# Scores ahead of a step's second layer, products with v behind it, in a two-bank buffer; two alternating banks for the first layer

## The chip, the cores and the metric

The kernel runs on one core of one Trainium2 chip. The metric is the device time of one execution in microseconds (us); lower is better. The kernel before is given by the median of three timed runs and by one further execution, from which the profile was taken.

## What is computed

The inputs are q, k and v of shape (batch 8, heads 8, sequence 576, head size 64) in float32, a norm vector of 512 and two feed-forward matrices of 512 x 2048 and 2048 x 512. Cut to what matters, the reference is:

```python
scores = q @ k.transpose(0, 1, 3, 2) / sqrt(64)
# heads 0-3: a query sees itself and the 31 keys before it
# heads 4-7: a query sees every earlier key whose position has the same remainder mod 32
attn = softmax(where(mask, scores, -1e9))
x = (attn @ v).transpose(0, 2, 1, 3).reshape(8, 576, 512)
xn = (x - mean(x)) / sqrt(var(x) + 1e-6) * g_ln
out = x + relu(xn @ w1) @ w2
```

## The kernel before

The 4608 tokens are cut into nine chunks of 512: chunk c < 8 is the first 512 tokens of batch entry c, and chunk 8 collects the last 64 tokens of all entries. The attention works on 32 "pairs" of two heads of one batch entry. Pairs with an even index are strided, those with an odd index local. The masks leave few blocks: a local pair has 18 score blocks for each head, each 32 queries by 64 keys; a strided pair has 11 for each head, each 64 rows by 54. These small float32 products run on tiles of TensorE (64 x 32 and 64 x 64), not on the full 128 x 128 array.

The first eight pairs are computed at the start, with chunk 0, in an order written out by hand (`ORDER`). Then comes the stretch that the change touches: chunks 1 to 6, each of 16 steps, 96 in all. Step f of chunk c does this in program order:

- **First layer**, `ffn1`: 12 matmuls of 128x128 by 512 columns into the PSUM bank `ph` (lines L802 and L809). There is one such bank, in the pool `ps_h`.
- ScalarE makes `hh` from `ph` (L814), then VectorE makes `hl` from `ph` and `hh` (L819). These two hold the first layer's result as a high and a low part.
- **One turn of the generator** `pieces()`, which threads the attention of the remaining 24 pairs through the steps.
- **Second layer**, `second(*prev)`: 12 matmuls (L829) with the `hh` and `hl` of the step before, into four banks `po` that a chunk holds for 16 steps. At step 0 the second layer ends the chunk before, and VectorE adds the residual (L835).

For i from 7 to 31 the generator makes a *visit*, of three steps where `short` holds and of four otherwise. `now` is pair i and `nxt` is pair i + 1. In the visit's first step `m_piece` runs: TensorE computes the scores of `nxt` (L445) and then, directly behind them, the product of `now`'s weights with v (L514). Both go into one buffer `m` of three banks. VectorE adds the mask (L473), takes the row maxima (L486), divides the product by its sums (L564); SyncE stores it; GpSimd subtracts the maxima (L491) and ScalarE takes the exponential (L497). The buffer is laid out so that head 0 and head 1 never use the same bank at the same time: for that the last score block of a strided pair lies in the third bank, the v products of head 0 lie in the third bank, and those of head 1 at the ends of the first two. The mask is added in three parts (strided) or two (local), the division is done in five.

In the visit's second step `x_raw` loads the stored output back in 32-column slices (ScalarE's queue, L593), `v_sums` makes the row sums (L534 to L536), `p_turned` turns the exponentials in 32x32 blocks and sends them to DRAM (L610, L614, buffer `pd`), `t_piece` turns the next raw q and k (L415, L416, L420), and `load_qk` fetches raw q and k of a later pair (L356). In the third step `p_load` brings the turned exponentials back as `pt` (L623 or L628; for a short visit with a strided `nxt` this stands in the second step, on SyncE's queue), and `x_blocks` turns `xraw` and splits it into the high and low part of the next chunk's x (L602, L685, L686).

Each engine runs its instructions in program order (a loop at the end of the kernel ties each to the one before it on its engine). The first visit has scores only, the last one products only; 24 visits have both. In chunk 6 a table `last_steps` adds work for the last two chunks at given steps: loads of the tail tokens, transposes and splits.

Of the kernel before, what the change touches and what calls it, by code (L numbers as in the profile page):

```python
# [8 lines left out]
F32 = mybir.dt.float32  # L9
# [53 lines left out]
def kernel(  # L63
# [10 lines left out]
    nc = tc.nc  # L74

    B, H, S, D = q.shape
    DM, DFF = w1.shape
    P = 128
# [5 lines left out]
    NL = (NB + 3) // 4  # L84
# [3 lines left out]
    CH = 512  # L88
# [20 lines left out]
    ps_h = ctx.enter_context(tc.tile_pool(name="ps_h", bufs=1, space=bass.MemoryType.PSUM))  # L109
# [198 lines left out]
    banks = [(ps_a, "a", 1024)]  # L308
    n_bank = [0]

    def bank(name):
        pool, tag, n = banks[n_bank[0] % len(banks)]
        n_bank[0] += 1
        return pool.tile([P, n], F32, tag=tag, name=name)

    def halves(ps, n, w):

        return ps.rearrange("p (h x) -> p h x", h=2)[:, :, 0:n * w].rearrange(
            "p h (t x) -> p h t x", x=w)
# [6 lines left out]
    class Pair:  # L326
# [97 lines left out]
        def s_blocks(self, ps):  # L424

            nt, w = self.nt, (64 if self.local else GS)
            wide = ps.shape[1] > 1024 and not self.local

            def at(h, t):
                o = 1024 + D * NL if wide and h == 0 and t == nt - 1 else 512 * h + w * t  # L430
                return ps[:, o:o + w]

            def block(n, h):
                rows = slice(64 * h, 64 * h + 64)
                if self.local:
                    t, jj = divmod(n, 4)
                    o = at(h, t)[STR * jj:STR * (jj + 1)]
                    lhsT = self.qt[rows, STR * n:STR * (n + 1)]
                    rhs, pos = self.kt[rows, STR * n:STR * n + 64], STR * jj
                else:  # L440
                    t, c = divmod(n, 2)
                    o = at(h, t)[64 * c:64 * c + 64]
                    lhsT = self.qt[rows, GS * n:GS * n + 64]
                    rhs, pos = self.kt[rows, GS * n:GS * (n + 1)], 64 * c
                nc.tensor.matmul(o, lhsT, rhs, start=True, stop=True, tile_position=(64 * h, pos))  # L445

            if self.local:
                n = 4 * NL if self.full else NB
            else:
                n = 2 * NS if self.full else NG  # L450
            for i in range(n):
                for h in range(2):
                    block(i, h)

            sv = halves(ps[:, 0:1024], nt, w)
            parts = [(r, 0, 2, t0, t1, sv[r, :, t0:t1]) for r, t0, t1 in self.parts]
            if wide:
                r = parts[1][0]
                parts[1:] = [(r, h, h + 1, nt - 1, nt, at(h, nt - 1)[r].rearrange(
                    "p (h t x) -> p h t x", h=1, t=1)) for h in range(2)]  # L460
            return parts

        def s_masked(self, parts):
            self.s_mask(parts)
# [73 lines left out]
        def v_blocks(self, ps):  # L538

            nt = self.nt  # L540

            def o(h, t):
                return 1024 + D * t if h == 0 else 512 * (t // 3) + 512 - D * (3 - t % 3 if t < 3 else nt - t)

            for i in range(NB if self.local else NG):
                for h in range(2):
                    self.v_block(i, h, lambda h, t: ps[:, o(h, t):o(h, t) + D], D)
            r = self.parts[1][0]
            parts = []
            for h, rs, t0, t1 in ((1, slice(0, P), 0, 3), (1, slice(0, P), 3, nt - 1), (1, r, nt - 1, nt),  # L550
                                  (0, slice(0, P), 0, nt - 1), (0, r, nt - 1, nt)):
                parts.append((rs, h, h + 1, t0, t1, ps[rs, o(h, t0):o(h, t0) + D * (t1 - t0)].rearrange(
                    "p (h t d) -> p h t d", h=1, d=D)))
            return parts

        def v_divide(self, parts):
            nt = self.nt
# [109 lines left out]
                nc.vector.tensor_tensor(  # L667
                    out=lo, in0=src, in1=hi.bitcast(F32), op=ALU.subtract)

    def m_piece(p, nxt):  # L670

        ps = bank(f"m{(p or nxt).id}")
        parts = nxt.s_blocks(ps) if nxt else None
        av = p.v_blocks(ps) if p else None
        if nxt:
            nxt.s_masked(parts)
        if p:
            p.v_divide(av)
            p.v_store()
        if nxt:  # L680
            nxt.s_sub()
            nxt.s_exp()

    def split_x(hi, lo, src):
        nc.scalar.activation(out=hi, in_=src, func=AF.Copy)  # L685
# [108 lines left out]
    def ffn1_high(c, f, ccs=range(NCC), ph=None):  # L794
        xh, xl = xt[c]
        new = ph is None
        if new:
            ph = ps_h.tile([P, CH], F32, tag="h", name=f"ph{c}_{f}")
        w1h = w1s[f][:, 0].rearrange("p (c f) -> p c f", c=NCC)
        for n, cc in enumerate(ccs):  # L800
            for i, x in enumerate((xh, xl)):
                nc.tensor.matmul(  # L802
                    ph, w1h[:, cc], x[:, cc, :], start=(new and n == 0 and i == 0), stop=False)
        return ph
# [18 lines left out]
    def ffn2(c, f, h, po):  # L823
        hh, hl = h
        w2h, w2l = (w2s[f][:, i] for i in range(2))
        for i in range(NT):
            cs = slice(i * P, (i + 1) * P)
            for n, (hx, w) in enumerate(((hh, w2h), (hh, w2l), (hl, w2h))):
                nc.tensor.matmul(  # L829
                    po[i], hx[:, cs], w,  # L830
                    start=(f == 0 and n == 0), stop=(f == NFC - 1 and n == 2))
# [15 lines left out]
    def second(c, f, h, xres):  # L847
        nonlocal po
        if f == 0 and c == NCHUNK - 1:
            po = [pool.tile([P, DM], F32, tag=tag, name=f"po{c}_{i}") for i, (pool, tag) in  # L850
                  enumerate(((ps_l, "x2"), (ps_h, "h"), (ps_l, "x3"), (ps_l, "x4")))]
        elif f == 0:
            po2 = [ps_o[i].tile([P, 1024], F32, tag="o", name=f"po{c}_{i}") for i in range(NT // 2)]
            po = [po2[i // 2][:, DM * (i % 2):DM * (i % 2 + 1)] for i in range(NT)]
        ffn2(c, f, h, po)
        if f == NFC - 1:
            finish(c, po, xres)
# [4 lines left out]
    ps, ph, hs, splits = {}, {}, {}, {}  # L862
# [143 lines left out]
    def pieces():  # L1006
        for i in range(2 * NHP - 1, NP):
            now = pairs[i] if i >= 2 * NHP else None
            nxt = pairs[i + 1] if i + 1 < NP else None
            short = i < 3 * NHP - 1 or i in (25, 27, 29)  # L1010
            m_piece(now, nxt)
            if i + 2 < NP:
                pairs[i + 2].load_v()
            yield
            if now:
                now.x_raw(nc.scalar)
            if nxt:
                nxt.v_sums()
                nxt.p_turned()
                if short and not nxt.local:  # L1020
                    nxt.p_load(nc.sync)
            if i + 2 < NP:
                pairs[i + 2].t_piece()
            if i + 3 < NP:
                pairs[i + 3].load_qk()
            yield
            if nxt and not (short and not nxt.local):
                nxt.p_load(nc.scalar)
            if now and now.b == B - 1:
                cc = now.h0 // 2  # L1030
                if cc >= NHP // 2:
                    whole_tile(0, (f"b21{cc % 2}", f"b11{cc % 2}"))
                now.x_blocks(whole[f"b{1 + cc // 2}1{cc % 2}"])
            elif now:
                now.x_blocks()
            yield
            if not short:
                yield

    gen = pieces()  # L1040
    RES_AT = 4, 5, 7, 8
    ps_r_ctx.close()
    ps_m_ctx = ExitStack()
    ps_m = ps_m_ctx.enter_context(tc.tile_pool(name="ps_m", bufs=1, space=bass.MemoryType.PSUM))
    banks[:] = [(ps_m, "m", 1536)]


    def tail(cc):
# [6 lines left out]
    wide = NCHUNK - 2  # L1055
# [44 lines left out]
    for c in range(1, wide):  # L1100
        xres = []
        for f in range(NFC):
            ph = ffn1(c, f)
            hh = h_high(c, f, ph)
            h = hh, h_low(c, f, ph, hh)
            next(gen, None)
            if c == wide - 1:
                for do in last_steps.get(f, ()):
                    do()
            second(*prev)  # L1110
            if 2 <= c < 2 + NFC // 4 and f in (2, 11):
                w_sums(2 * (c - 2) + int(f > 2))
            if 2 <= c < 2 + NFC // 4 and f in (3, 15):
                w_whole(2 * (c - 2) + int(f > 3))
            if f in RES_AT:
                xres.append([x_load(c, RES_AT.index(f))])
            if f - 3 in RES_AT:
                i = RES_AT.index(f - 3)
                xres[i].append(x_scale(xres[i][0], f"{c}_{i}"))
            prev = c, f, h, xres  # L1120
# [139 lines left out]
```

## Time and profile before

| what | value |
|---|---|
| median of three runs | 887.09 us (886.63 to 887.17) |
| the profiled execution's own time | 885.76 us |
| its span, first to last instruction | 884.0 us |
| TensorE matmul busy | 866.6 us, 98% of the span |
| VectorE busy | 484.9 us, 55% |
| ScalarE busy | 213.1 us, 24% |
| GpSimd busy | 211.4 us, 24% |
| mean granted TensorE clock | 0.998 of full speed |

The span is what the trace covers; 1.76 us of the execution's own time lie outside of it. Busy times of different engines overlap. A matmul's row is longer (about 390 ns) than the distance between two matmuls (about 227 ns), since they are pipelined, so the distance between starts, not the row's length, is what a matmul costs.

### The profile page before, as it was taken

Reading aid. Unit: us, or ns where it says so; the run is one execution under the profiler, and the core shown is the slowest. Engines: PE = TensorE matmul, PEld = TensorE weight load, DVE = VectorE, ACT = ScalarE, POOL = GpSimd, SP = SyncE. Lnnn points to the kernel's source line nnn. Section 1 sums busy time; section 2 is a strip of 40 time slices with the busy share of each in tenths; the row PEclk is TensorE's granted clock in tenths of the full one; section 3 lists DMA queues with packets and bytes.
Section 4 is the critical chain, followed back from the end, with each engine's and each line's share of the span. In section 5 each row is a group of like instructions: output and inputs, shape, how many; then the busy total and the mean of one; then the engine's idle time right before and its main releaser. Section 6 shows DMA issues by size and latency. Waiting matters only on the chain.

```text
span 884.0 us, 18492 instructions
## 1 busy us (share of the span) xinstructions
PE 866.6 (98%) x7405; PEld 712.4 (81%) x7405; DVE 484.9 (55%) x933; ACT 213.1 (24%) x351; POOL 211.4 (24%) x246
## 2 busy tenths in 40 slices
PE   7799999999999999999999999999999999999997
PEld 6588888888888888888888888888887888888886
DVE  5899975456354645455544545565564542434442
ACT  3786741111111111111111111111112221212121
POOL 5887850011030223013301302113002111121000
PEclk9999999999999999999999999999999999999999
DMA  9999754685678575856686577758774153321111
GB/s 190 197 302 264 253 110 101 127 165 130 115 190 157 117 155 137 184 121 123 131 210 126 131 137 205 138 122 162 184 135 94 48 193 112 99 85 49 52 45 47
DMA packets 368301, 124.73 MB, mean 141 GB/s; under 512 B 296404, under 2 KB 353880, under 8 KB 368216
## 3 DMA queue, kind: packets, MB, share of 16 engines
q1 hardware_dynamic: 291160, 109.46, 51.0%
q10 hardware_dynamic: 77056, 14.10, 9.0%
q8 instruction: 58, 0.95, 0.5%
q14 instruction: 27, 0.22, 0.1%
HBM read 84.90 MB, written 38.60 MB: 140 GB/s over the span
## 4 chain that ended last, share of the span: by engine, by line
PE 92%; DMA 2%; SPq 2%; DVE 2%; issue 0%; ACT 0%; POOL 0%; ACTq 0%; DVEq 0%; POOLq 0%
PE po L829 43%; PE ph L802 22%; PE ph L809 11%; PE x L1144 9%; PE m L514 2%; PE m L445 2%; SPq L401 1%; DMA v_s<-in_v_dram 1%; PE av L514 1%; DMA rows<-in_q_dram 1%; PE t L373 0%; PE px L636 0%; PE cm L286 0%; DMA pt<-pd 0%; PE s L445 0%
## 5 line engine op out<-in xcount | busy, mean ns | idle before, releaser
L829 PE MATMUL po<-w,hh 128*128 128x512 f32 x1152 | 358.9, 393 | 0.0
L829 PEld LDWEIGHTS po<-w,hh 128*128 128x128 f32 x1152 | 213.5, 188 | 45.0
L829 PE MATMUL po<-w,hl 128*128 128x512 f32 x576 | 224.3, 389 | 0.0
L819 DVE SCALAR_TENSOR_TENSOR hl<-ph,hh 128x512 fp32r<-128x512 f32 x112 | 77.2, 689 | 210.9 <-ACT hh L814 210.6
L802 PE MATMUL ph<-xh,w 128*128 128x512 f32 x444 | 174.3, 393 | 0.6 <-DVE hl L819 0.6
L802 PE MATMUL ph<-xl,w 128*128 128x512 f32 x444 | 172.9, 389 | 0.0
L814 ACT ACTIVATE hh<-ph 128x512 fp32r<-128x512 f32 x112 | 66.7, 596 | 316.0 <-PE ph L809 261.5
L829 PEld LDWEIGHTS po<-w,hl 128*128 128x128 f32 x576 | 108.1, 188 | 23.0
L809 PE MATMUL ph<-xh,w 128*128 128x512 f32 x444 | 118.9, 390 | 0.0
L491 POOL TENSOR_TENSOR sm<-sm,mx 128x640 f32<-128x640 f32 (+1 forms) x31 | 39.3, 1268 | 316.6 <-DVE mx L486 284.0
L802 PEld LDWEIGHTS ph<-xh,w 128*128 128x128 f32 x444 | 83.4, 188 | 18.3 <-DVE hl L819 1.0
L809 PEld LDWEIGHTS ph<-xh,w 128*128 128x128 f32 x444 | 83.2, 188 | 17.4
L802 PEld LDWEIGHTS ph<-xl,w 128*128 128x128 f32 x444 | 83.4, 188 | 17.0
L722 POOL TENSOR_TENSOR rs<-rs,mhalf 128x1 f32<-128x1 f32 x36 | 19.8, 549 | 231.4 <-DVE rs L721 231.3
L497 ACT ACTIVATE sm<-sm 128x648 f32<-128x648 f32 (+1 forms) x32 | 23.8, 744 | 107.5 <-POOL sm L491 107.4
L303 POOL TENSOR_TENSOR w<-r,w 128x512 fp32r<-128x512 f32 x29 | 37.9, 1315 | 7.9 <-ACT w L299 7.6
L1097 POOL TENSOR_TENSOR rings<-stage,rings 128x512 fp32r<-128x512 f32 x16 | 20.6, 1289 | 71.0 <-ACT rings L1096 71.0
L1144 PE MATMUL x<-half_t,rings 128*128 128x512 f32 x144 | 36.4, 389 | 0.0
L1144 PEld LDWEIGHTS x<-half_t,rings 128*128 128x128 f32 x144 | 27.0, 188 | 5.6
L686 DVE TENSOR_TENSOR xl<-xo,xh 128x512 fp32r<-128x512 f32 x20 | 13.8, 692 | 27.6 <-ACT xh L685 27.6
L486 DVE TENSOR_REDUCE mx<-sm 128x12 f32<-128x648 f32 (+1 forms) x32 | 26.3, 823 | 2.4
L564 DVE TENSOR_TENSOR xo<-m,den 64x64 f32<-64x64 f32 (+3 forms) x120 | 27.1, 289 | 0.0
(148 smaller groups left out, 870.7 us busy)
## 6 DMA issues: line engine op xcount, KB each, us to landing
s<-in_moe_w_ch_dram SPq DMA_DIRECT2D x32, 512.0 KB
out_dram<-x SPq DMA_DIRECT2D x32, 256.0 KB
raw<-in_q_dram SPq DMA_DIRECT2D x108, 72.0 KB
raw<-in_k_dram SPq DMA_DIRECT2D x108, 72.0 KB
wd<-w SPq DMA_DIRECT2D x24, 256.0 KB
ringa<-wd SPq DMA_DIRECT2D x24, 256.0 KB
xds<-xo SPq DMA_DIRECT2D x32, 162.0 KB
v_l<-in_v_dram SPq DMA_DIRECT2D x32, 144.0 KB
```

The lines of the kernel that those rows point to most:

```text
L303: eng.tensor_tensor(out=t[:, 1], in0=self.w[i], in1=t[:, 0].bitcast(F32), op=ALU.subtract)
L486: nc.vector.reduce_max(mx[:, :, 0:nt], sm, axis=AX.X)
L491: eng.tensor_tensor(out=sm, in0=sm, in1=mx[:, :, 0:nt].unsqueeze(3).broadcast_to([P, 2, nt, sm.shape[3]]), op=ALU.subtract)
L497: nc.scalar.activation(out=self.smv, in_=self.smv, func=AF.Exp, scale=SCALE)
L514: nc.tensor.matmul(at(h, t)[m * j:m * (j + 1)], self.p_cols(rows, t, j), self.v[rows, n, 0:w], start=True, stop=True, tile_position=(64 * ...
L564: nc.vector.tensor_tensor(out=xo[r, t0:t1, h0:h1].rearrange("p t h d -> p h t d"), in0=av, in1=den[r, h0:h1, t0:t1].unsqueeze(3).broadcast_to(
L802: nc.tensor.matmul(ph, w1h[:, cc], x[:, cc, :], start=(new and n == 0 and i == 0), stop=False)
L809: nc.tensor.matmul(ph, w1l[:, cc], xt[c][0][:, cc, :], start=False, stop=(cc == NCC - 1))
L814: nc.scalar.activation(out=hh, in_=ph, func=AF.Relu)
L819: nc.vector.scalar_tensor_tensor(out=hl, in0=ph, scalar=0.0, in1=hh.bitcast(F32), op0=ALU.max, op1=ALU.subtract)
L829: nc.tensor.matmul(po[i], hx[:, cs], w, start=(f == 0 and n == 0), stop=(f == NFC - 1 and n == 2))
L1144: nc.tensor.matmul(ps, wx, xx, start=(start and j == 0 and i == 0), stop=(j == 1 and i == 2), skip_group_check=not start)
```

## The change

The turn of the generator is split: it now takes a turn ahead of the second layer and one behind it, and a visit has six or eight such half steps instead of three or four steps. The scores of `nxt` (`s_piece`) stay between first and second layer of the visit's first step. The v products of `now` (`v_piece`), their division and store and the load of v for a later pair stand behind the second layer of that step. `p_turned`, now ahead of `v_sums`, stays ahead of the second layer of the second step, with the short strided `p_load`; `x_raw`, `t_piece` and `load_qk` go behind that step's second layer. The other `p_load` stays ahead of the second layer of the third step, `x_blocks` goes behind it.

Scores and products are two allocations, one after the other, in one buffer of two banks, head 0 in the first and head 1 in the second. The mask is then added in two parts for either kind, the division done in two. The bank that becomes free is a second bank for the first layer: from chunk 1 on odd steps use `ps_b`, even ones `ps_h`.

```diff
         def s_blocks(self, ps):
             def at(h, t):
-                o = 1024 + D * NL if wide and h == 0 and t == nt - 1 else 512 * h + w * t
-                return ps[:, o:o + w]
+                return ps[:, 512 * h + w * t:512 * h + w * (t + 1)]
...
         def v_blocks(self, ps):
             def o(h, t):
-                return 1024 + D * t if h == 0 else 512 * (t // 3) + 512 - D * (3 - t % 3 if t < 3 else nt - t)
+                return 512 * h + D * t
...
-    def m_piece(p, nxt):
-
-        ps = bank(f"m{(p or nxt).id}")
-        parts = nxt.s_blocks(ps) if nxt else None
-        av = p.v_blocks(ps) if p else None
-        if nxt:
-            nxt.s_masked(parts)
-        if p:
-            p.v_divide(av)
-            p.v_store()
-        if nxt:
-            nxt.s_sub()
-            nxt.s_exp()
+    def s_piece(p):
+        p.s_masked(p.s_blocks(bank(f"s{p.id}")))
+        p.s_sub()
+        p.s_exp()
+
+    def v_piece(p):
+        p.v_divide(p.v_blocks(bank(f"av{p.id}")))
+        p.v_store()
...
-            ph = ps_h.tile([P, CH], F32, tag="h", name=f"ph{c}_{f}")
+            ph = (ps_b if c and f % 2 else ps_h).tile([P, CH], F32, tag="h", name=f"ph{c}_{f}")
...
-            m_piece(now, nxt)
+            if nxt:
+                s_piece(nxt)
+            yield
+            if now:
+                v_piece(now)
             if i + 2 < NP:
                 pairs[i + 2].load_v()
             yield
+            if nxt:
+                nxt.p_turned()
+                nxt.v_sums()
+                if short and not nxt.local:
+                    nxt.p_load(nc.sync)
+            yield
             if now:
                 now.x_raw(nc.scalar)
-            if nxt:
-                nxt.v_sums()
-                nxt.p_turned()
-                if short and not nxt.local:
-                    nxt.p_load(nc.sync)
             if i + 2 < NP:
                 pairs[i + 2].t_piece()
...
             if nxt and not (short and not nxt.local):
                 nxt.p_load(nc.scalar)
+            yield
...
             yield
             if not short:
                 yield
+                yield
...
-    banks[:] = [(ps_m, "m", 1536)]
+    ps_m, ps_b = (ps_m_ctx.enter_context(tc.tile_pool(name=n, bufs=1, space=bass.MemoryType.PSUM))
+                  for n in ("ps_m", "ps_b"))
+    banks[:] = [(ps_m, "m", 1024)]
...
             second(*prev)
+            next(gen, None)
```

## Rows read from the trace of the kernel before

**Rows 1.** The 96 steps: length, busy us (instructions) PE, PEld, DVE, ACT, POOL, PEclk, DMA.

```profile
141.10:712.75 571.65, 570.52 (x5089) 468.93 (x5089) 302.59 (x616) 96.01 (x155) 93.45 (x101) 1.00 0.64 140
```

**Rows 2.** Waits of TensorE in that stretch: total us, times, longest us.

```profile
PE ph L802 <- DVE hl L819: 0.6, 1, 0.6
PE m L514 <- DMA pt<-pd: 0.5, 1, 0.5
```

**Rows 3.** Chain of work, a plain step, then one with scores and products: start, us.

```profile
398.57 1.81 PE ph L802 x8
...
404.01 1.81 PE ph L802 x8
405.82 0.91 PE ph L809 x4
406.73 0.84 PE m L445 x44
407.56 0.90 PE m L514 x58
408.47 2.94 PE po L829 x12
411.41 1.81 PE ph L802 x8
```

**Rows 4.** The same chain in the first visit, which has scores only.

```profile
141.10 1.81 PE ph L802 x8
...
143.81 0.84 PE m L445 x44
144.65 2.94 PE po L829 x12
147.60 1.81 PE ph L802 x8
```

**Rows 5.** The same chain in the last visit, which has products only.

```profile
675.32 0.91 PE ph L809 x4
676.22 0.90 PE m L514 x58
677.12 2.99 PE po L829 x12
680.11 1.81 PE ph L802 x8
```

**Rows 6.** Timeline of VectorE behind the scores that start at 406.66.

```profile
407.45 0.69 DVE L819 SCALAR_TENSOR_TENSOR hl<-ph,hh 128x512 fp32r<-128x512 f32 x1 [3.74 <-ACT hh L814]
408.53 0.95 DVE L473 TENSOR_TENSOR sm<-m,mask_s 128x540 f32<-128x540 f32 x3 [0.38 <-PE m L514]
...
410.33 1.06 DVE L564 TENSOR_TENSOR xo<-m,den 128x192 f32<-128x192 f32 x5
```

**Rows 7.** Timeline of SyncE's queue in a short visit with a strided `now`.

```profile
202.63 0.79 SPq L582 DMA_DIRECT2D xds<-xo  x2
203.52 5.22 SPq L401 DMA_DIRECT2D v_s<-in_v_dram  x6
210.51 1.83 SPq L614 DMA_DIRECT2D pd<-sm  x4
```

**Rows 8.** Timeline of ScalarE and its queue in that visit.

```profile
209.24 1.93 ACTq L593 DMA_DIRECT2D xraw<-xds  x4
211.27 0.60 ACT L814 ACTIVATE hh<-ph 128x512 fp32r<-128x512 f32 x1 [5.38 <-DMA xraw<-xds]
214.00 0.36 ACTq L623 DMA_DIRECT2D pt<-pd  x1
```

**Rows 9.** Timeline of VectorE at the end of that visit.

```profile
213.61 0.71 DVE L602 STREAM_TRANSPOSE xo<-xraw 128x512 f32<-128x512 f32 x1 [1.01 <-DMA xraw<-xds]
...
216.80 0.69 DVE L819 SCALAR_TENSOR_TENSOR hl<-ph,hh 128x512 fp32r<-128x512 f32 x1
```

**Rows 10.** Timeline of VectorE at a chunk's end: the four residual adds.

```profile
435.21 2.71 DVE L835 SCALAR_TENSOR_TENSOR x<-po,rs,x 128x512 f32<-128x512 f32 x4
```

More of the change, by code (lines that the diff above doesn't have):

```diff
@@ L426, in s_blocks @@
             nt, w = self.nt, (64 if self.local else GS)
-            wide = ps.shape[1] > 1024 and not self.local
             def at(h, t):
-                o = 1024 + D * NL if wide and h == 0 and t == nt - 1 else 512 * h + w * t
-                return ps[:, o:o + w]
+                return ps[:, 512 * h + w * t:512 * h + w * (t + 1)]
             def block(n, h):
@@ L453, in s_blocks @@
                     block(i, h)
[L455 to L461, printed above, removed]
+            sv = halves(ps, nt, w)
+            return [(r, 0, 2, t0, t1, sv[r, :, t0:t1]) for r, t0, t1 in self.parts]
         def s_masked(self, parts):
@@ L547, in v_blocks @@
                     self.v_block(i, h, lambda h, t: ps[:, o(h, t):o(h, t) + D], D)
[L548 to L554, printed above, removed]
+            at = halves(ps, nt, D)
+            return [(r, 0, 2, t0, t1, at[r, :, t0:t1]) for r, t0, t1 in self.parts]
         def v_divide(self, parts):
@@ L1043 @@
     ps_m_ctx = ExitStack()
-    ps_m = ps_m_ctx.enter_context(tc.tile_pool(name="ps_m", bufs=1, space=bass.MemoryType.PSUM))
-    banks[:] = [(ps_m, "m", 1536)]
+    ps_m, ps_b = (ps_m_ctx.enter_context(tc.tile_pool(name=n, bufs=1, space=bass.MemoryType.PSUM))
+                  for n in ("ps_m", "ps_b"))
+    banks[:] = [(ps_m, "m", 1024)]
     def tail(cc):
```

## The prediction

> **What bounds the kernel now.** I first read the windows view over the 96 steps that the change touches, to see whether any engine but TensorE matters there. It does not: TensorE is busy 570.52 of 571.65 us at the full granted clock, VectorE about half of it, ScalarE and GpSimd a sixth [rows 1]. Then the list of waits: TensorE waits twice in the whole stretch, 0.6 us for an `hl` and 0.5 us for a `pt`, 1.1 us together [rows 2]. That is the most that a better order of the other engines can give back. What is left to ask is how long TensorE's own work becomes, so I read the chain of work step by step. A plain step goes from 398.57 to 404.01, 5.44 us, that is 2.72 for each layer. A step with scores and products goes from 404.01 to 411.41, 7.40 us, so the small products cost 1.96 us: 0.84 for the scores, 0.90 for the products with v, and 0.22 because the second layer behind them takes 2.94 instead of 2.72 [rows 3].
>
> **The change part by part.**
>
> *Two runs of small tiles instead of one.* The same matmuls are issued, so the two runs keep their lengths. What changes is how often TensorE goes from the full array to small tiles and back: once for a visit today, twice afterwards, in 24 visits. The trace shows each run alone. The first visit has scores only: its step goes from 141.10 to 147.60, 6.50 us, 1.06 over a plain one, of which the run is 0.84 and the second layer's excess 0.22 again [rows 4]. The last visit has products only: from 675.32 to 680.11 pass 4.79 us, where a plain step needs 0.91 and 2.72, 3.63; that is 1.16 over [rows 5, 3]. Apart they cost 2.22 us, together 1.96: a visit that is split costs 0.26 more. Of this, 0.05 is the second layer of the last visit (2.99 against 2.94 us), which belongs to no entry or exit; without it 0.21. The value I take is 0.22, the excess of a full layer behind a small run, which then falls on the next step's first layer too. 24 x 0.22 = +5.3 us; ends 24 x 0.21 = 5.0 and 24 x 0.26 = 6.2. Only strided scores and local products are seen alone; I assume the same for the other kind. This work is on the engine that sets the end, and nothing covers it.
>
> By the Trainium skill, TensorEngine Tiling (Array Packing), section Key Properties, changing the tiling mode drains TensorE. Scores and products use different tilings, so by that rule a visit has three changes today (full to scores, scores to products, products to full) and four afterwards; were all priced alike at half of the 0.22 us, the split would add 24 x 0.11 = 2.6 us where the rows give 5.3.
>
> *The wait of the products for the mask.* The products now go into the same buffer as the scores and must wait until VectorE has added the mask, which today they need not. In the step shown, the scores start at 406.73 and end at 407.56; `hl` runs from 407.45 to 408.14, the mask takes 0.95 in three parts and would start right behind `hl` (today it waits 0.38 for the products) [rows 3, 6]. It would end by 409.1. The products are due 2.94 us after the scores, at 410.5. That leaves 1.4 us, so I take nothing; were VectorE later than that, the second run and all full layers queued behind it on TensorE would wait. The places with least room are the two short visits with a strided `now`, since `x_blocks` moves half a step towards the next scores and already runs without a pause into the `hl` ahead of the mask: turned at 213.61, `hl` at 216.80 [rows 9]. Today 216.80 is just when `hl` is due (0.8 us after the scores start, as in rows 6). `x_blocks` becomes later by what its data does: the output is divided behind the second layer, some 0.7 us later than today, because today the division (1.06 us in five parts) stands behind mask and maximum anyway [rows 6]. So `hl` and mask are late by 0.7 there, half of the room.
>
> *The queues that steps are moved past.* SyncE: the store and the six v loads take 0.79 and 5.22 us and stand ahead of `pd` today as well [rows 7]; starting 0.7 us later they end at about 209.4, and `pd`, which goes out at 210.51 today, is not pushed back. `p_turned` ahead of `v_sums` makes it earlier, if anything. ScalarE: `x_raw` issues at 209.24 once the store has landed and takes 1.93 us; 0.7 us later it makes the next `hh` (211.27, already held back by it today) later by about as much [rows 8]. That `hh` feeds a second layer one step, 5.4 us, later, so it costs nothing. `p_load` keeps its place, 214.00 [rows 8], while the products are due half a step, 2.7 us, later: the 0.5 us wait for `pt` goes. `t_piece` moves half a step in the text, but VectorE is in order and has nothing in between except the row sums, so it hardly moves. At a chunk's end the division now stands behind four residual adds, 2.71 us [rows 10]; these start when the second layer ends, as the products do, so the division comes some 2 us later there, still ahead of the next `hl`.
>
> *Fewer parts.* Mask and division lose one and three instructions for a visit. VectorE is at 302.59 of 571.65 us [rows 1]; worth nothing on the path.
>
> *Two banks for the first layer.* The next first layer need not wait for `hl` of the step before. This wait occurs once, 0.6 us [rows 2]; I take all of it, the other bound is none. The second layer's need for `hl` comes 2.7 us later than the wait did, so it doesn't take its place.
>
> **Sum.** 5.3 - 0.5 - 0.6 = +4.2 us. Against the profiled execution's own 885.76 us (span 884.0 and 1.76 around it) that is 890.0. The three timed runs have a median of 887.09, 1.33 us above the profiled one, and the time to be forecast is one of theirs: 887.09 + 4.2 = 891.3 us.
>
> **The rivals.**
>
> *The turn into small tiles costs per change of tiling* (the rule above, as a mechanism of this kernel): the 0.22 us would be the price of two of them, the way in and the way out, 0.11 each; the split adds two and leaves out the one from scores to products, so one is added, 24 x 0.11 = 2.6 us, less 1.1: +1.5, 888.6 us, no change that can be measured. It decides below (1.8 + 1.1) / 24 = 0.12 us for a split visit. Against it: the scores take 0.84 us before products [rows 3] as before a full layer [rows 4], and the products 0.90 behind scores [rows 3] as behind a full layer [rows 5], so the change between the two has no price to be saved. Were the split free altogether, the two waits alone would make 887.09 - 1.1 = 886.0, still within 0.2%. 0.14, most of it without measurable change.
>
> *VectorE is late with the mask.* The products wait at the two short visits with a strided `now`, or everywhere. With VectorE 1.4 us over its room at those two, on top of the forecast: 891.3 + 2.8 = 894.1; with half a microsecond at all 24: 891.3 + 12 = 903. It decides from the point where the mask ends 1.4 us later than worked out above. For it: the zero pause of rows 9. Against it: in the trace before, `hl` comes 0.8 us after the start of the scores even there [rows 9, 6]. 0.14.
>
> *The split costs as forecast and VectorE or the DMA queues hide it*: excluded, as TensorE has only 1.1 us of waits to give [rows 2].
>
> **How the numbers follow.** My forecast has 0.72: 890.0 (the low price of 5.0 and both waits gone, 891.0, less a microsecond for the scatter between medians) to 893.3 (6.2, no wait gone). The first rival's 888.6 is taken in at the low end, the second's 894.1, nearly, at the high end: 888.6 to 894.0. A measurement of this kernel can tell about 0.2%, 1.8 us, from no change. Faster by more: 0.03, only if the split costs nothing and something unseen is gained. Within: 0.12, from the first rival and the low edge of the forecast. Slower: 0.85.
>
> **What would show it.** In the chain of the changed kernel, scores and products stand in different half steps with 0.84 to 0.91 us each, and both the second layer behind the scores and the first layer behind the products show about 0.22 us over 2.72. A four-step visit becomes 0.2 to 0.26 us longer. The waits of TensorE list neither `pt` nor `hl`. Mask and products: the mask starts right behind `hl`, and ends a microsecond or more ahead of the products. I am wrong if a layer behind a small run shows no excess, if TensorE waits for VectorE ahead of the products, or if a visit keeps its length.

## The result, and the profile after

The changed kernel takes 892.1 us (median of 5 runs, 890.25 to 893.1), the kernel before on the same chip 887.17 (886.63 to 888.24): a ratio of 1.0051, 95% interval 1.0035 to 1.0066 (ratio and interval are taken over all runs, so the ratio is not exactly that of the medians). Taken again in a later experiment it was 1.0046 (1.0031 to 1.0061). It is slower by about half a per cent; 891.3 us was forecast.

The profiled execution took 893.1 us with a span of 891.2, which is 7.2 us more than the span of before. Not all of that is the change, so I cut the span in three: the opening up to the first layer of chunk 1, the 96 steps, and the end. These are the windows of the changed kernel, with the columns of [rows 1]:

```profile
144.40:720.00 575.60, 575.60 (x5089) 467.12 (x5089) 297.62 (x532) 96.11 (x155) 93.41 (x101) 1.00 0.63 139
0.00:144.40 144.40, 133.08 (x1586) 109.50 (x1587) 117.36 (x209) 85.50 (x141) 94.71 (x122) 0.96 0.86 206
720.00:891.20 171.20, 165.91 (x732) 137.10 (x731) 64.64 (x108) 32.66 (x55) 23.64 (x23) 1.00 0.27 86
```

The 96 steps take 575.60 us against 571.65 [rows 1]: +3.95. The opening took 144.40 against 141.10, where the program is the same; it varies from one execution to the next (142.45 in the second profile of the changed kernel, experiment 7), and it is as long in kernels that keep one run in a visit (143.40 in experiment 1, 144.54 in experiment 6). The mean granted clock of the opening was 1.00 in the profile of before, 0.99 in that of experiment 7 and 0.96 in all others. The end is the same to 0.1 us (171.20 against 171.25). From here on the length of the 96 steps is the measure: in both profiles of the changed kernel it is 575.60 exactly. TensorE is now busy in all of it, 575.60 of 575.60: both waits of [rows 2] are gone, and yet the stretch is longer.

The chain of work of the changed kernel, the step that answers to [rows 3], and the next visit's:

```profile
409.27 1.81 PE ph L785 x8
411.08 0.91 PE ph L792 x4
411.99 0.83 PE s L443 x44
412.83 2.94 PE po L812 x12
415.77 0.90 PE av L507 x58
416.67 2.07 PE ph L785 x8
418.74 0.92 PE ph L792 x4
419.66 2.72 PE po L812 x12
...
435.98 0.90 PE s L443 x58
436.88 2.97 PE po L812 x12
439.84 0.84 PE av L507 x44
...
459.96 0.84 PE s L443 x44
```

Two things stand out. The runs of small products have kept their lengths: 0.83 and 0.90 here, 0.84 and 0.90 in [rows 3]. And one more full layer pays: the second layer behind the scores takes 2.94 as before, and now the first layer behind the products takes 2.07 + 0.92 = 2.99 in place of 2.72, which it took in [rows 3] (1.81 + 0.91). The chain of the kernel before, where its next two visits begin behind the scores at 406.73 [rows 3]:

```profile
430.45 0.90 PE m L445 x58
...
454.20 0.84 PE m L445 x44
```

From scores to scores a visit of four steps takes 435.98 - 411.99 = 23.99 us and then 459.96 - 435.98 = 23.98; before it took 23.72 and then 23.75. That is 0.27 for the visit with strided scores and 0.23 for the one with local scores.

VectorE behind the scores, in the timeline of the changed kernel; it answers to [rows 6]:

```profile
412.72 0.69 DVE L802 SCALAR_TENSOR_TENSOR hl<-ph,hh 128x512 fp32r<-128x512 f32 x1 [3.63 <-ACT hh L797]
413.33 0.88 DVE L466 TENSOR_TENSOR sm<-s,mask_s 128x540 f32<-128x540 f32 x2
414.31 0.83 DVE L479 TENSOR_REDUCE mx<-sm 128x12 f32<-128x648 f32 x1
416.73 0.88 DVE L552 TENSOR_TENSOR xo<-av,den 128x512 f32<-128x512 f32 x2 [1.60 <-PE av L507]
```

The mask starts right behind `hl` and ends at 414.21. The products start at 415.7, so they have 1.5 us of room; in all 23 visits that have both it is 1.49 to 1.65. VectorE has become faster on its work (the mask in two parts takes 0.88 where three took 0.95, the division 0.88 where five took 1.06) and this is worth nothing, since it then sits idle for 1.60 us until the products are there.

### The profile page after: what moved, and what is told of

The parts are those of the page before. It is cut to its first block, busy times and chain, and to the rows that moved or that the text cites. A ratio compares the mean times of both kernels' runs of the same rounds, so it can differ in the third digit from the quotient of the medians.

```text
span 891.2 us, 18428 instructions
## 1 busy us (share of the span) xinstructions
PE 874.6 (98%) x7405; PEld 713.7 (80%) x7405; DVE 479.6 (54%) x849; ACT 214.3 (24%) x351; POOL 211.8 (24%) x246
## 4 chain that ended last, share of the span: by engine, by line
PE 94%; DMA 2%; DVE 1%; SPq 1%; issue 1%; ACT 0%; ACTq 0%; DVEq 0%
PE po L812 44%; PE ph L785 23%; PE ph L792 11%; PE x L1136 9%; PE av L507 3%; PE s L443 3%; DMA s<-in_moe_w_ch_dram 1%; DMA rows<-in_k_dram 1%; DMA rows<-in_q_dram 1%; SPq L366 0%; PE cm L286 0%; PE pp L494 0%; DVE x L818 0%; PE px L624 0%; DVE p L263 0%
## 5 line engine op out<-in xcount | busy, mean ns | idle before, releaser
L785 PE MATMUL ph<-xh,w 128*128 128x512 f32 x444 | 177.5, 400 | 0.0
L792 PE MATMUL ph<-xh,w 128*128 128x512 f32 x444 | 119.1, 390 | 0.0
L552 DVE TENSOR_TENSOR xo<-av,den 64x128 f32<-64x128 f32 (+3 forms) x56 | 29.8, 567 | 30.1 <-PE av L507 29.9
L818 DVE SCALAR_TENSOR_TENSOR x<-po,rs,x 128x512 f32<-128x512 f32 x36 | 24.6, 744 | 3.4 <-PE po L812 3.3
```

Source lines behind the costliest of these rows:

```text
L552: nc.vector.tensor_tensor(out=xo[r, t0:t1, h0:h1].rearrange("p t h d -> p h t d"), in0=av, in1=den[r, h0:h1, t0:t1].unsqueeze(3).broadcast_to(
L785: nc.tensor.matmul(ph, w1h[:, cc], x[:, cc, :], start=(new and n == 0 and i == 0), stop=False)
L792: nc.tensor.matmul(ph, w1l[:, cc], xt[c][0][:, cc, :], start=False, stop=(cc == NCC - 1))
```

## The experiments

The theory is that a second run of small tiles in a visit costs TensorE its way in and out, and that everything else gives back at most the two waits. Its rival is that the moved work, the buffer or the alternating banks cost the time. All medians of experiments 1 to 4 stand against 887.65 us of the kernel before (15 runs), those of 5 to 7 against 887.61 (17 runs). The column "96 steps" is read from the windows view of each.

| kernel | runs of small tiles in a visit | median us | ratio (95%) | 96 steps us |
|---|---|---|---|---|
| before | 1 | 887.17 | | 571.65 |
| changed | 2 | 892.1 | 1.0051 (1.0035 to 1.0066) | 575.60 |
| 1, joined runs | 1 | 888.49 | 1.0005 (0.9996 to 1.0015) | 572.56 |
| 2, split only | 2 | 893.31 | 1.0062 (1.0049 to 1.0074) | 577.38 |
| 3, one h bank | 2 | 894.06 | 1.0071 (1.0058 to 1.0084) | 577.53 |
| 4, three runs | 3 | 902.53 | 1.0164 (1.0150 to 1.0178) | 586.14 |
| 5, products at once | 1, with a stop in it | 922.62 (one run) | | 605.74 |
| 6, no waits | 1 | 886.99 | 0.9990 (0.9979 to 1.0000) | 570.73 |
| 7, changed again | 2 | 892.1 | 1.0046 (1.0031 to 1.0061) | 575.60 |

**1. The new placement without the split.** The kernel before, with the half steps of the changed one for all but the products:

```diff
             m_piece(now, nxt)
+            yield
             if i + 2 < NP:
                 pairs[i + 2].load_v()
             yield
-            if now:
-                now.x_raw(nc.scalar)
             if nxt:
-                nxt.v_sums()
                 nxt.p_turned()
+                nxt.v_sums()
...
+            yield
+            if now:
+                now.x_raw(nc.scalar)
             if i + 2 < NP:
                 pairs[i + 2].t_piece()
...
             second(*prev)
+            next(gen, None)
```

> The kernel before with the half-step placement of the changed one for everything but the products: scores and products stay one run in the three-bank buffer, and the first layer keeps one bank. Theory (the added time is the second run of small tiles, 23 visits at about 0.24 us): the chain shows one run in a visit and the 96 steps take 570 to 572 us as before; time 886 to 887.5 us against 887.2. Rival (the moved work on the other engines or the buffer costs the time): about 892 us, as the changed kernel.

As a time it can't be told from before, and it is far from the 892 us of the rival: that is out for the moved steps. Both numbers lie a little above what I had written down, though: 888.49 us against at most 887.5 (the kernel before beside it had 887.65), and these steps against at most 572:

```profile
143.40:715.96 572.56, 571.15 (x5089) 469.60 (x5089) 307.16 (x616) 96.13 (x155) 93.97 (x101) 1.00 0.65 140
```

The two waits are still there:

```profile
PE m L514 <- DMA pt<-pd: 0.8, 1, 0.8
PE ph L802 <- DVE hl L819: 0.6, 1, 0.6
```

The chain shows where the one for `pt` comes from. SyncE's queue stands for 1.6 us ahead of `pd`, until a load of v has landed, and `pt` is fetched when `pd` has landed:

```profile
209.78 3.42 DMA v_s<-in_v_dram
213.23 0.43 SPq L614
...
214.38 2.01 DMA pd<-sm
...
216.45 3.48 DMA pt<-pd
219.98 0.97 PE m L514 x58
```

The kernel before has the same chain: its queue stands for 1.7 us ahead of `pd` in the same way, and the products begin at 217.45. `x_raw`, which ScalarE has issued by 213.62, is not in it. A later due time of the products is one way to lose this wait; experiment 6 loses it with the products as early as before.

**2. The split without the rest.** The kernel before, products behind the second layer, in the old three-bank buffer, with the old parts and one bank for the first layer:

```diff
-            m_piece(now, nxt)
+            if nxt:
+                ps, parts = s_piece(now, nxt)
+            else:
+                ps = bank(f"m{now.id}")
+            yield
+            if now:
+                now.v_divide(now.v_blocks(ps))
+                now.v_store()
             if i + 2 < NP:
                 pairs[i + 2].load_v()
             yield
...
+            yield
+            if now:
+                now.x_raw(nc.scalar)
...
```

> The kernel before with the products behind the second layer, still in the three-bank buffer, mask and division still in three and five parts, one bank for the first layer (the store, the load of v and x_raw follow the products by half a step). Theory: the split alone makes nearly all the difference, 23 x 0.24 = 5.5 us less a 0.5 us wait for pt: 891 to 893 us. Rival (two banks, parts or alternating first layer carry it): 887 to 888 us.

```profile
142.88:720.26 577.38, 576.46 (x5090) 466.62 (x5089) 302.30 (x616) 95.83 (x155) 93.40 (x101) 1.00 0.64 139
```

The split alone brings the whole loss: 577.38 us for the steps, 4.82 more than experiment 1 and 5.73 more than before. The rival that the two banks, the parts or the alternation carry it is out. The median lies 0.3 us over what I expected. Two waits, 0.6 us for an `hl` and 0.3 for a residual add, are in it.

**3. The alternating banks.** The changed kernel with one bank for the first layer:

```diff
-            ph = (ps_b if c and f % 2 else ps_h).tile([P, CH], F32, tag="h", name=f"ph{c}_{f}")
+            ph = ps_h.tile([P, CH], F32, tag="h", name=f"ph{c}_{f}")
```

> The changed kernel with one bank for the first layer; the eighth bank lies empty. Theory: the second bank is worth at most the one wait for hl of the kernel before, 0.6 us and the slower layer behind it, 0.3: 892 to 893 us. Rival (alternating banks is what pays back part of the split): 2 us or more slower than the changed kernel.

The steps take 1.93 us more than in the changed kernel, twice what the theory allowed and just under the rival's 2: the second bank pays back more than the wait of before. The median lies 1 us over the 893 that I had as the upper end. There are now two waits for `hl`, and the chain shows where one of them comes from:

```profile
442.43 5.57 DMA xds<-xo
448.00 0.03 ACTq L581
448.02 0.04 issue
448.06 2.03 DMA xraw<-xds
450.09 0.03 issue
450.12 0.61 ACT hh L797
450.73 0.02 issue
450.75 0.70 DVE hl L802
451.46 0.04 issue
451.50 2.11 PE ph L785 x8
453.61 0.91 PE ph L792 x4
```

The store of a pair lands at 448.0. `x_raw` waits for it on ScalarE, and `hh` stands behind `x_raw`; `hl` needs `hh`, and with one bank the next first layer needs `hl`. The changed kernel has the same hold-up of `hh` (450.07 there, after 5.74 us in which ScalarE computed nothing and at the end issued `x_raw`), and TensorE does not notice, because the next first layer writes the other bank. A layer behind such a wait is also slower, 2.11 + 0.91 = 3.02 against 2.72, and 2.14 + 0.92 behind the other wait, so that 1.3 us of waits become 1.9.

**4. A third run.** The changed kernel with the scores cut in halves, the first half behind the second layer of the step ahead:

```diff
...
+    def s_begin(p):
+        begun[p] = bank(f"s{p.id}")
+        p.s_blocks(begun[p], 0)
...
     def s_piece(p):
-        p.s_masked(p.s_blocks(bank(f"s{p.id}")))
+        if p in begun:
+            p.s_masked(p.s_blocks(begun.pop(p), 1))
+        else:
+            p.s_masked(p.s_blocks(bank(f"s{p.id}")))
...
+            if short and i + 2 < NP:
+                s_begin(pairs[i + 2])
             yield
             if not short:
                 yield
+                if i + 2 < NP:
+                    s_begin(pairs[i + 2])
                 yield
```

> The changed kernel with the scores of 23 visits cut once more: the first half of the blocks runs half a step earlier, behind the second layer of the step ahead, the rest where it was. Nothing else moves. Theory (each run of small tiles has a price of 0.22 to 0.27 us for its way in and out): 23 x 0.22 to 0.27 = 5.1 to 6.2 us more than the changed kernel, 897 to 898 us. Rival (the added time is a wait of the products for the mask or another engine): no more than the changed kernel, 892 us.

TensorE waits for nothing in these 96 steps, 586.14 of 586.14 us busy, so the rival is out; but the steps are 10.54 us longer, 0.46 for each of 23 cuts, and not the 0.22 to 0.27 that I expected; the time of 902.53 us lies well over my 898. The window and the chain:

```profile
143.69:729.83 586.14, 586.14 (x5090) 467.43 (x5089) 297.56 (x532) 96.06 (x155) 93.36 (x101) 1.00 0.62 137
```

```profile
413.62 0.49 PE s L443 x20
414.11 2.05 PE ph L794 x8
416.16 0.92 PE ph L801 x4
417.08 0.50 PE s L443 x24
417.58 2.97 PE po L821 x12
420.54 0.90 PE av L507 x58
```

The first layer behind the half run takes 2.97, 0.25 more than 2.72, as expected. In addition the two halves take 0.49 + 0.50 where the whole took 0.83, 0.16 more: it looks as if a run had a fixed part, which a cut inside of one kind of products pays twice. For the local scores it is 0.56 + 0.56 against 0.90, 0.22 more, and the first layer between their halves has 0.27 too much. That is 0.41 for each of 11 strided visits and 0.49 for each of 12 local ones, 10.4 of the 10.54 us.

**5. Why the products can't simply follow in two banks.** The changed kernel with the products directly behind the scores:

```diff
             if nxt:
                 s_piece(nxt)
-            yield
             if now:
                 v_piece(now)
+            yield
```

> The changed kernel with the products of a visit directly behind its scores, in the same two-bank buffer, so that they wait for the mask with nothing between. Theory: the buffer makes the products wait until VectorE has added the mask (in the changed kernel the scores end at 412.76 and the mask at 414.21), so TensorE stands still some 1.5 to 1.9 us in each of 23 visits: 34 to 44 us, less 23 x 0.24 = 5.5 us for nothing else changing in the runs if the entry in between is saved; 920 to 932 us, and the list of waits names VectorE. Rival (the order of the runs, not the second layer between them, keeps the products from waiting): 892 us or less.

```profile
425.68 0.86 PE s L443 x44
426.54 1.46 issue
427.99 0.96 PE av L507 x53
```

TensorE stands still for 1.46 us between the two, while VectorE finishes `hl` and adds the mask:

```profile
427.01 0.88 DVE L466 TENSOR_TENSOR sm<-s,mask_s 128x540 f32<-128x540 f32 x2
```

The list of waits has 33.1 us in 23 visits, but names VectorE for 11 of them only (L473 is the fill behind a local mask):

```profile
PE av L507 <- issue: 16.3, 11, 1.5
PE av L507 <- DVE sm L473: 15.4, 11, 1.4
PE av L507 <- DMA raw<-in_k_dram: 1.4, 1, 1.4
```

The times decide it: in every one of the 23 visits the products start 0.10 to 0.11 us after the mask ends. TensorE's busy time falls to 572.66 us, near that of a joined run. So the two-bank buffer does make the products wait for the mask, and the second layer in between is what covers this in the changed kernel.

**6. A joined run without the two waits.**

```diff
             if nxt:
-                nxt.v_sums()
                 nxt.p_turned()
+                nxt.v_sums()
...
-            next(gen, None)
             if c == wide - 1:
                 for do in last_steps.get(f, ()):
                     do()
+            next(gen, None)
```

> The kernel before with two orders changed: p_turned ahead of v_sums, and in chunk 6 the entries of last_steps ahead of the generator's turn instead of behind it. Scores and products stay one run. Theory (only the two waits and the slower layer behind each can be had, 1.5 us in all): the 96 steps take 570 to 571 us against 571.65, the list of waits there is empty or shorter, and the time is 885.5 to 887 us, which may not be told from 887.2 with certainty. Rival: the waits come from elsewhere and stay, 887 us.

No wait is left in the 96 steps, and they take 570.73 us, all of it busy:

```profile
144.54:715.27 570.73, 570.73 (x5089) 469.50 (x5089) 305.02 (x616) 96.25 (x155) 93.68 (x101) 1.00 0.64 140
```

That is 0.92 us less than before, and without a split. How much of it is due to the new order is not shown. The wait for `pt` hangs on the loads of v on SyncE's queue (experiment 1), and their issue ahead of `pd` took 2.86 us here, against 5.22 before [rows 7] and 5.42 in experiment 1, which has the same order of `p_turned` and `v_sums` and kept the wait. The median of 886.99 us is the lowest of all, but the interval against before reaches to 1.0000, so as a time the gain of 0.1% is not settled, and the steps are those of one profile. It is also the clean partner of the changed kernel: both without a wait, one run against two, 570.73 against 575.60.

**7. The changed kernel again.**

> The changed kernel once more, for a second profile and more timed runs beside the kernel before. Theory: the 96 steps take 575.6 us again within 0.3, since their order is fixed by TensorE; the time before them, which the change does not touch, differs (141.1 us in the profile of before, 144.4 in that of the changed kernel); so the time is 891 to 892.5 us. Rival (the change itself lengthens the opening): the steps start at 144.4 us again, or later.

```profile
142.45:718.05 575.60, 575.60 (x5089) 466.77 (x5089) 297.79 (x532) 96.25 (x155) 93.58 (x101) 1.00 0.64 139
```

The steps take 575.60 us once more, and the opening 142.45 instead of 144.40. So the opening scatters by 2 us with the same kernel, and no part of it is shown to come from the change; the kernel of experiment 6, with one run, had the longest of all, 144.54.

## Why the prediction held, point by point

*The bound.* That only TensorE's own work counts, and that 1.1 us of waits is all that can be given back, held: without waits the steps take 570.73 us, 0.92 less than before. What the sum left out is the slow layer behind a wait, 0.3 us each time in experiment 3.

*The price of the split.* Forecast 24 x 0.22 = 5.3 us, measured 575.60 - 570.73 = 4.87. The count in it was wrong: of the 25 visits one has scores only and one products only, so 23 are split, not 24 (the same slip stands in the description of the kernel). With 23 the forecast's price gives 5.1, and the measured one is 0.21 a visit. That this is so near the 0.22 is in part luck. Visit against visit the split costs 0.27 with strided scores and, where the joined visit is a plain one of 23.75 us, 0.23 with local ones, 5.7 us or so in all. But the joined visits are not all alike: in six of the twelve with local scores the step takes 7.55 to 7.58 us in experiment 6, where the others take 7.41 to 7.46, mostly because the strided products behind the scores take longer:

```profile
433.54 0.90 PE m L445 x58
434.44 0.97 PE m L514 x44
```

They take 0.97 to 1.02 in these visits, 0.85 to 0.88 in the others, and 0.84 apart. By moving away from the scores they give back nearly 0.9 us of the price. Why they are long, and only in some visits, was not tried. That the excess would sit in the second layer behind the scores and in the first layer behind the products was right, 2.94 and 2.99; I had put 2.94 for the latter. The 0.05 that I took off the 0.26 of the rows, as belonging to no entry or exit, is this difference: a full layer behind local products takes 2.99 where they run alone.

*The rule that each change of tiling costs alike.* It would have added 2.6 us. Strided scores and local products keep their lengths, 0.83 and 0.90, whether together or apart, and the measured 4.87 is nearly twice that: the rival is out as a forecast. Local scores and strided products do give something back when they part, as said above, but in some visits far more than in others, so it is not one price for a change either. Experiment 4 shows what in the rule was right. The Trainium skill, TensorEngine Tiling (Array Packing), section Key Properties, says that changing the mode drains TensorE. A run that is cut inside one kind of products pays 0.16 to 0.22 us more in the runs themselves, while the cut between strided scores and local products pays nothing there; that agrees with a fixed part that each kind pays already in the joined run. By the measured numbers the changes are not alike, however.

*The products' wait for the mask.* Nothing, as forecast, with 1.5 us of room where I had 1.4. I had half of it at the two short visits with a strided `now`, and this was wrong: the room behind them is 1.50 and 1.49 as well. In the later of them `x_raw` was issued 1.6 us earlier in the visit than before, not 0.7 later, and VectorE had been idle for 1.33 us ahead of the `hl` in question. Experiment 5 shows that the dependence is real.

*The queues.* `pd` was not pushed back and the wait for `pt` went, as forecast. I had read the loads of v as out of the way of `pd`, however, and in the kernel before they hold it up (experiment 1). That a later `hh` "costs nothing" was right for the changed kernel, but for another reason than I gave: I named the second layer's slack, and experiment 3 shows that the next first layer would have waited; the second bank is the cover.

*Two banks for the first layer.* Mis-sized: taken at 0.6 us, worth 1.93 in the new order. In the sum this does not show, because in the new order there would have been more to lose.

*The sum.* +4.2 forecast, +3.95 measured for the steps, +4.9 and +4.5 between the medians of the two comparisons. The scatter of the opening is as large as what remains between these.

## What to carry to other kernels

When the engine that sets the end is busy 99.8% of a stretch, a better order of the other engines can give back little more than the waits in its list; ask first what the new order does to that engine's own instructions. Small products on parts of TensorE's array are best kept in one run: here every further run costs 0.23 to 0.27 us on the layers next to it (0.21 net of what some products gave back), and 0.46 us when a run of one kind is cut. A spare bank is worth what it covers in the order that it is used in, which the waits of the old order do not tell.

## What I had not expected of the hardware

A run of small products behaves as if it had a fixed part: 44 score instructions take 0.83 us, 20 of them 0.49 and 24 of them 0.50. And a full layer behind a run of local products, or behind a wait, does not recover with its first matmul. In the changed kernel that first start is 0.34 us ahead of the second, and from 416.94 to 418.58 the next starts are 0.234 us apart; in experiment 3, behind the wait, they are 0.230 apart from 451.84 to 453.22; in a plain layer, from 409.33 to 410.92, they are 0.227 apart. The granted clock is 1.00, the 2.4 GHz level, in the 96 steps of both. The second layer behind the strided scores does not show it (0.228). What it comes from was not tried and stays open.
